# A planner's priorities replaced by a table of ranks, and a weight load tied to the other operand of pair 4

## The chip, the cores and the metric

The kernel runs on one core of one Trainium2 chip. The metric is the device time of one execution in microseconds (us); the shorter, the better. Three runs of the kernel before gave 262.81, 263.26 and 263.25 us, median 263.25.

## What is computed

The reference is a sparse attention followed by a feed-forward layer. There are 4 batches, 8 heads, 768 positions and a head size of 64.

```
k_rep = k.reshape(B, H, 12, 64, D).mean(axis=3)        # one mean key per block of 64
gate  = q @ k_rep^T, causal by blocks                   # each query picks its 3 best blocks and its own
attn  = softmax(mask(0.125 * q @ k^T))                  # only picked blocks, and causal
x     = (attn @ v) as 3072 tokens x 512
out   = gelu_tanh(x @ w_in) @ w_out                     # 512 -> 2048 -> 512, fp32 out
```

## The kernel before, in words

Heads are handled in pairs, four pairs to a batch, sixteen in all; pairs 0 to 3 are batch 0. Each pair goes through these steps.

- **Loads** (`load`, issued on the queue of SyncE, SP): k, q and v of the pair. In batch 0 they arrive as they lie, most of them in rooms inside the tiles G and TS; from pair 4 on k and q arrive in a layout that VectorE can transpose in blocks (`emit_t`, L278). Pair 0 is loaded in halves by `load_0` (L303) from two queues.
- **Preparation** (`pre`): in batch 0 TensorE turns k and q with an identity matrix (L417, L420). Block sums of k give gate scores (L542). VectorE adds the constant cgate (L565), takes the eight largest (L574), compares with the third (L575), and combines the result with the constant ownm into an additive mask (L579). TensorE or a DMA transposes the mask (L611, L618), and it is copied into place (L247, L243). The constants come from `consts` on GpSimd (POOL): cgate and ownm in `gates` (L354 to L365), block indicators in `e16` (L372, L375), and four sets of memsets (L383 to L387), one for each of four buffers.
- **Heads**: scores into a two-bank PSUM tile called wide (L715 in `heads2` for batch 0, L898 in `heads` for the others), exp on ScalarE (L734, L911), a causal select on the diagonal by POOL (L760, L925), the product with v (L783, L937), normalisation on VectorE (L801, L802; L820, L821), and a transpose into xT (L840, or the DMA of L845). There are two wide tiles and six buffers for the exponentials (`at`).
- **Stage one** (`s1`): x @ w_in, 128 matmuls of 384 columns to a batch (L973), with gelu on ScalarE (L985) into G. It shares the two wide tiles with the scores.
- **Stage two**: for batch 0 plain (`s2_plain`, L1055, 96 matmuls). The plain matmuls of the first output tile need the first half of w_out from their first step on. Batches 1 to 3 use a scheme with seven products instead of eight (`s2`, L1103, 168 matmuls to a batch), whose sums VectorE makes (`sums` L1043, `w_sums` L1025) and whose results it joins (L1147).

The table of exp and that of gelu are switched by a small activation (L681); ScalarE does it twice to a batch.

**Weights and queues.** `load_w` (L333, L336) is issued by POOL. Ahead of the first half of each weight it copies 16 elements of a tile of the last load it is to follow (L333, the tiles `after_in` and `after_out`): POOL waits there until that load has landed, and what stands behind it in POOL's order waits too. w_in follows v of pair 3, w_out follows k of pair 4. `hold` (L344) puts a tiny DMA on SP's queue that reads the first half of a weight, so that SP issues nothing further until it has landed: held_in stands before the loads of pair 4, held_out before the later ones. `fill` (L393) issues eight DMAs on SP that copy the block indicators under kT.

**The order of the work.** No order is written by hand. Every step is an `Op` with its engines and a planned duration on each, its dependencies, the buffers that it takes and gives, and a priority. `Plan.solve` is a list scheduler: at each turn it looks at all steps that could start, keeps those that start within 0.03 us of the earliest, and takes the one with the lowest priority number (a planned DMA goes by the time at which it became ready). The plan's start times then give the order in which instructions are emitted, and each engine runs its own instructions strictly in that order. Buffers, and the engine of steps that may run on several, are chosen by the plan as well. Priorities in the kernel before are formulas, such as `1000 * b + 600 + n` for stage one and `1e6` for `warm`.

`warm` (L1200) adds 72 matmuls of 256 columns with an identity whose results nobody reads. Their priority is the worst, so that the plan puts them where TensorE would find nothing else; all 72 are always emitted, and each takes a PSUM bank for its time.

Of the kernel before, what the change touches and what calls it, by code (L numbers as in the profile page):

```python
# [15 lines left out]
MASKVAL = 28672.0  # L16
NEGBIG = -1.0e9
SCALE = 0.125


class Op:
# [13 lines left out]
class Plan:  # L35
# [12 lines left out]
    def add(self, *a, **kw):  # L48
        op = Op(*a, **kw)
        self.ops.append(op)  # L50
        return op
# [81 lines left out]
def kernel(  # L133
# [16 lines left out]
    HP = H // 2  # L150
# [59 lines left out]
    for i in range(NB):  # L210
# [3 lines left out]
                     for h in range(2)])  # L214
# [3 lines left out]
    plan = Plan({  # L218
        **{kind: ([tuple(persist.tile([128] + dims, dt, name=f"{kind}_{n}_{m}")
                         for m, (dims, dt) in enumerate(parts))  # L220
                   for n in range(most)], most)
           for kind, most, parts in (
               ("at", 6, [([1024], FP16)]),
               ("osb", 2, [([2, 2, HD], FP32)]),
               ("ksd", PF, [([NC * 2 * 64], FP32)]),
               ("qsd", PF, [([NC * 2 * 64], FP32)]),
# [24 lines left out]
    ld = {}  # L251
# [75 lines left out]
    def load_w(name, dst, src, part, deps, prio, after=None):  # L327
        view = src.rearrange("(i p) f -> p i f", p=128)

        def emit(_):  # L330
            if after is not None:
                x = const.tile([1, 16], FP32, name=f"after_{name}")
                nc.gpsimd.tensor_copy(out=x, in_=T[after][0:1, 0, 0, 0:16]  # L333
                                      if len(T[after].shape) == 4 else
                                      T[after][0:1, 0, 0:16])
            nc.gpsimd.dma_start(out=dst[part], in_=view[part])  # L336
        go = add({POOL: 1.0}, emit, deps, prio=prio)
        issued[name] = go
        return add({"DMA": 6.0}, lambda _: None, [go], prio=prio, lag=1.6)

    def hold(name, src, dep):
        def emit(_):
            x = const.tile([1, 16], FP16, name=f"held_{name}")
            nc.sync.dma_start(out=x, in_=src[0:1, 0, 0:16])  # L344
        return add({SP: 0.5}, emit, [dep], prio=-1)
# [350 lines left out]
    def heads2(p):  # L696
# [3 lines left out]
        for ui, unit in enumerate(units(p)):  # L700
# [30 lines left out]
            def ex_e(_, u=u, n=n):  # L731
# [5 lines left out]
                        "p (h w) -> p h w", h=2)[:, :, 0:n],  # L737
                    func=AF.Exp, bias=0.0, scale=SCALE)
            ex = add({ACT: 0.13 + 2 * n * 0.000833}, ex_e,
# [137 lines left out]
    def heads(p):  # L877
# [4 lines left out]
        for h in range(2):  # L882
            pvs = []
            for gi, (ja, jb) in enumerate(groups):
# [24 lines left out]
                def ex_e(_, u=u, n=wa + wb):  # L909
# [3 lines left out]
                        in_=plan.buf[("st",) + u][:, 0:n],  # L913
                        func=AF.Exp, bias=0.0, scale=SCALE)
                ex = add({ACT: 0.84}, ex_e,
# [279 lines left out]
    def warm():  # L1195
        z = ident16.unsqueeze(1).to_broadcast([128, 2, 128])
        on = add({"NONE": 0.0}, lambda _: None, [], -1e6, lag=1.3)
        for n in range(NWARM):
            def emit(_, n=n):
                nc.tensor.matmul(plan.buf["warm", n][:, 0:256], ident16, z,  # L1200
                                 start=True, stop=True)
            add({PE: 0.215 if n < NCOLD else 0.107}, emit, [on], 1e6,
                takes=("warm", ("warm", n)),
                gives=[("warm", n)])
# [24 lines left out]
    for x in range(2):  # L1229
        w_ready["out", x] = load_w(  # L1230
            "out", w_out16, moe_w_out,
            (every, slice(NF // 2 * x, NF // 2 * (x + 1)), every),
            [ld["k", HP]], 40, None if x else ("k", HP))
    held.append(hold("out", w_out16, w_ready["out", 0]))
    for p in range(HP):
        heads2(p)
# [12 lines left out]
    for p in range(HP, NPAIR):  # L1249
# [4 lines left out]
        if hp == HP - 1:  # L1254
            s1(b)
            s2(b)
    warm()
    order = plan.solve()
    with tc.manual_schedule():
        for op in order:  # L1260
# [31 lines left out]
```

## Time and profile before

| What | us |
|---|---|
| median of three runs | 263.25 |
| time of the profiled execution | 262.67 |
| its span in the profile | 261.0 |
| TensorE busy (matmul) | 253.7 |
| TensorE weight loads | 176.2 |
| VectorE busy | 177.8 |
| ScalarE busy | 164.4 |
| GpSimd busy | 80.8 |

The span is the time from the first to the last thing that the profiler saw on the core; what the profiled execution took beyond it lies around it. A row such as "40.43 0.83 PE L1200 MATMUL ... x6" of the timeline is: start, length of the run of equal instructions, engine, line of the kernel, operation, tiles, count. In a row of groups the numbers behind the bar are busy time, mean of one instruction in ns, and idle time of the engine just before them with what ended it. In the table of stages each engine has its busy time and, in brackets, its instructions; the last three columns are the granted clock of TensorE, the share of the DMA engines and GB/s.

### The profile page before, as it was taken

Reading aid. Unit: us, or ns where it says so; the run is one execution under the profiler, and the core shown is the slowest. Engines: PE = TensorE matmul, PEld = TensorE weight load, DVE = VectorE, ACT = ScalarE, POOL = GpSimd, SP = SyncE. Lnnn points to the kernel's source line nnn. Section 1 sums busy time; section 2 is a strip of 40 time slices with the busy share of each in tenths; the row PEclk is TensorE's granted clock in tenths of the full one; section 3 lists DMA queues with packets and bytes.
Section 4 is the critical chain, followed back from the end, with each engine's and each line's share of the span. In section 5 each row is a group of like instructions: output and inputs, shape, how many; then the busy total and the mean of one; then the engine's idle time right before and its main releaser. Section 6 shows DMA issues by size and latency. Waiting matters only on the chain.

```text
span 261.0 us, 6531 instructions
## 1 busy us (share of the span) xinstructions
PE 253.7 (97%) x2542; PEld 176.2 (68%) x2542; DVE 177.8 (68%) x527; ACT 164.4 (63%) x207; POOL 80.8 (31%) x165
## 2 busy tenths in 40 slices
PE   6999999999999999999999999999999999999994
PEld 5777776565564655656677888656777887656883
DVE  2978737506598999989988999997534353345543
ACT  2366887666898696575799920666899912665000
POOL 8657634002374383120057820200044400000000
PEclk9999999999999999999999999999999999999999
DMA  8997999999999999899979913211004122000222
GB/s 163 219 215 148 187 194 134 178 185 192 163 194 173 190 189 203 156 179 164 178 124 169 193 56 116 97 28 25 3 1 143 34 80 84 0 0 3 80 83 80
DMA packets 130816, 32.63 MB, mean 125 GB/s; under 512 B 124544, under 2 KB 126688, under 8 KB 130784
## 3 DMA queue, kind: packets, MB, share of 16 engines
q1 hardware_dynamic: 126048, 27.62, 53.0%
q0 software_dynamic: 3136, 4.19, 9.9%
q10 hardware_dynamic: 1600, 0.39, 0.8%
q8 instruction: 20, 0.33, 0.5%
q14 instruction: 12, 0.10, 0.1%
HBM read 27.26 MB, written 6.29 MB: 129 GB/s over the span
## 4 chain that ended last, share of the span: by engine, by line
PE 85%; ACT 6%; DVE 6%; issue 2%; POOL 1%; DVEq 0%; POOLq 0%; ACTq 0%
PE wide L973 32%; PE bank L1103 20%; PE wide L898 7%; PE bank L1055 7%; ACT at L911 5%; PE bank L937 5%; PE bank L1200 3%; PE wide L715 3%; PE bank L542 2%; PE bank L783 2%; PE bank L420 1%; PE bank L417 1%; PE bank L840 1%; PE bank L611 1%; POOL at L925 1%
## 5 line engine op out<-in xcount | busy, mean ns | idle before, releaser
L973 PE MATMUL wide<-xT,w_in 128*128 128x384 f16 x512 | 85.9, 326 | 0.0
L985 ACT ACTIVATE G<-wide 128x768 f16<-128x768 f32 x64 | 51.8, 810 | 40.0 <-PE wide L973 40.0
L973 PEld LDWEIGHTS <-w_in 128*128 128x128 f16 x512 | 49.4, 98 | 32.7 <-issue 1.5
L911 ACT ACTIVATE at<-wide 128x896 f16<-128x896 f32 x72 | 60.7, 915 | 3.6 <-PE wide L898 2.2
L925 POOL TENSOR_SCALAR_AFFINE_SELECT at<-at 128x256 f16<-128x256 f16 x72 | 29.7, 416 | 64.1 <-ACT at L911 63.3
L898 PE MATMUL wide<-qT,kT 76*128 76x512 f16 (+1 forms) x192 | 38.9, 305 | 0.3 <-DVE qT L247 0.2
L1147 DVE TENSOR_TENSOR osb<-bank,osb 128x512 f32<-128x512 f32 (+1 forms) x36 | 22.3, 619 | 12.9 <-PE bank L1103 12.8
L1103 PEld LDWEIGHTS <-G 128*128 128x128 f16 x288 | 27.3, 98 | 5.2 <-issue 0.3
L1103 PE MATMUL bank<-w_out,G 128*128 128x256 f16 x216 | 30.5, 272 | 0.0
L937 PEld LDWEIGHTS <-at 128*128 128x128 f16 x504 | 23.6, 97 | 5.9 <-POOL at L925 1.8
L734 ACT ACTIVATE at<-wide 128x1024 f16<-128x1024 f32 (+3 forms) x24 | 21.2, 917 | 9.1 <-PE wide L715 8.8
L937 PE MATMUL bank<-v,at 128*128 128x65 f16 x504 | 26.5, 194 | 0.1
L1055 PE MATMUL bank<-w_out,G 128*128 128x512 f16 x96 | 25.1, 379 | 0.4 <-DVE osb L247 0.4
L245 POOL CAST kT<-k 64x768 f16<-64x768 f32 x17 | 14.4, 845 | 29.1 <-DVE k L436 28.6
L1103 PEld LDWEIGHTS <-XS 128*128 128x128 f16 x216 | 20.5, 98 | 3.4 <-DVE XS L1043 0.2
L898 PEld LDWEIGHTS <-kT 76*128 76x128 f16 x192 | 15.6, 97 | 9.7 <-issue 1.4
L1103 PE MATMUL bank<-TS,XS 128*128 128x256 f16 x144 | 20.3, 272 | 0.0
L1043 DVE TENSOR_TENSOR XS<-G 128x768 f16<-128x768 f16 x12 | 6.5, 552 | 18.1 <-ACT G L985 18.1
L436 DVE STREAM_TRANSPOSE k<-ksd 128x768 f32<-128x768 f32 x12 | 11.5, 962 | 9.1 <-DMA ksd<-in_k_dram 9.0
L245 POOL CAST v<-vsd 128x768 f16<-128x768 f32 x13 | 11.1, 851 | 18.6 <-DMA vsd<-in_v_dram 18.6
L1200 PE MATMUL bank<-ident 128*128 128x256 f16 x72 | 12.3, 302 | 2.1 <-DVE ident L175 2.1
L821 DVE TENSOR_TENSOR xn<-bank,zr 128x384 f16<-128x384 f32 x24 | 13.4, 558 | 0.8
(99 smaller groups left out, 323.8 us busy)
## 6 DMA issues: line engine op xcount, KB each, us to landing
out_dram<-osb SPq DMA_DIRECT2D x24, 256.0 KB
vsd<-in_v_dram SPq DMA_DIRECT2D x26, 192.0 KB
ksd<-in_k_dram SPq DMA_DIRECT2D x48, 96.0 KB
qsd<-in_q_dram SPq DMA_DIRECT2D x48, 96.0 KB
w_in<-in_moe_w_in_dram POOLq DMA_DIRECT2D x2, 1024.0 KB, 10.7
w_out<-in_moe_w_out_dram POOLq DMA_DIRECT2D x2, 1024.0 KB, 12.7
G<-in_k_dram SPq DMA_DIRECT2D x4, 192.0 KB
G<-in_q_dram SPq DMA_DIRECT2D x4, 192.0 KB
```

Source lines behind the costliest of these rows:

```text
L245: nc.gpsimd.tensor_copy(out=out, in_=in_)
L734: nc.scalar.activation(out=T["at", u][:, :, 0:n], in_=plan.buf[("st",) + u].rearrange("p (h w) -> p h w", h=2)[:, :, 0:n], func=AF.Exp, bi ...
L898: nc.tensor.matmul(st[:, x:e], kT16[i][h][0:76, s0:s0 + 128], qT16[i][h][0:76, s0 + (x - cb):s0 + (e - cb)], start=True, stop=True)
L911: nc.scalar.activation(out=T["at", u][:, 0:n], in_=plan.buf[("st",) + u][:, 0:n], func=AF.Exp, bias=0.0, scale=SCALE)
L925: nc.gpsimd.affine_select(out=dg, in_=dg, compare_op=ALU.is_ge, fill=0.0, base=0, pattern=[[0, 2], [1, 128]], channel_multiplier=-1)
L937: nc.tensor.matmul(pvv[:, qc, 0:65], at[:, cb + (qc - jc) * 128: cb + (qc - jc + 1) * 128], v16[i][:, jc, h, :], start=(gi == 0 and jc == ...
L973: nc.tensor.matmul(hps[:, 512 * e:512 * e + HALF], w_in16[:, ci, (2 * j + e) * 128: (2 * j + e + 1) * 128], T["xT", b][:, ci, HALF * h:HAL ...
L985: nc.scalar.activation(out=G[:, :, h, j, :], in_=plan.buf["hps", b, j, h].rearrange("p (e w) -> p e w", e=2)[:, :, 0:HALF], func=AF.Gelu_a ...
L1055: nc.tensor.matmul(plan.buf["ops", b, ti], G[:, f % 2, 2 * ti // NC, f // 2, ti % (NC // 2) * 128:ti % (NC // 2) * 128 + 128], w_out16[:, ...
L1103: nc.tensor.matmul(dst[:, HD * h:HD * h + HD], FACT[m][0][:, j, t * 128:(t + 1) * 128], FACT[m][1][:, j, :], start=(clear and j == 0), sto ...
L1147: nc.vector.tensor_tensor(out=dst(), in0=src(), in1=other(), op=ALU.add)
L1200: nc.tensor.matmul(plan.buf["warm", n][:, 0:256], ident16, z, start=True, stop=True)
```

## The change

A list of integers, RANK, is put at the head of the file, one for each step of the plan in the order in which the steps are added. After all steps have been added, each step's priority is overwritten with its rank; the last 72, the fillers, all have the worst rank, 1684. The scheduler, the planned durations and the steps themselves stay. The ranks come from a search made outside the kernel, which also replayed each plan with late loads.

The dependency of the w_out load, and the tile that `after_out` reads, become q of pair 4 in place of k of pair 4. In the code q of a pair is added after k.

```diff
+RANK = [
+    186, 144, 143, 173, 141, 142, 315, 164, 439, 154, 164, 553, 307, 165,
...
+    1684, 1684, 1684, 1684]
...
         w_ready["out", x] = load_w(
             "out", w_out16, moe_w_out,
             (every, slice(NF // 2 * x, NF // 2 * (x + 1)), every),
-            [ld["k", HP]], 40, None if x else ("k", HP))
+            [ld["q", HP]], 40, None if x else ("q", HP))
     held.append(hold("out", w_out16, w_ready["out", 0]))
...
     warm()
+    assert len(RANK) == len(plan.ops)
+    for op, rank in zip(plan.ops, RANK):
+        op.prio = rank
     order = plan.solve()
```

A line of the kernel before stands 147 lines further down in the kernel after, and 150 behind the new loop.

## The prediction

> **What bounds the kernel now.** I read the page's busy shares first, then the chain that ended last, then the table of stages, then the timeline.
>
> ```profile
> span 261.0 us, 6531 instructions
> PE 253.7 (97%) x2542; PEld 176.2 (68%) x2542; DVE 177.8 (68%) x527; ACT 164.4 (63%) x207; POOL 80.8 (31%) x165
> PEclk9999999999999999999999999999999999999999
> DMA  8997999999999999899979913211004122000222
> PE 85%; ACT 6%; DVE 6%; issue 2%; POOL 1%; DVEq 0%; POOLq 0%; ACTq 0%
> L1200 PE MATMUL bank<-ident 128*128 128x256 f16 x72 | 12.3, 302 | 2.1 <-DVE ident L175 2.1
> ```
>
> The reader is to see that TensorE carries both the busy time and 85% of the chain, at full clock, and that 72 of its matmuls (L1200) compute nothing: they multiply an identity and are never read. Because matmul ends are modelled, I measured PE from start to start. A row of twelve of them ends 1.47 us after it begins and a single one takes 0.27, so the pitch is (1.47 - 0.27)/11 = 0.109 us; the 48 stage-one matmuls of L973 that take 7.96 us give (7.96 - 0.33)/47 = 0.162. The stages:
>
> ```profile
> 10.00:20.00 10.00, 9.91 (x142) 7.51 (x142) 7.95 (x39) 6.31 (x9) 5.37 (x12) 1.00 1.18 217
> 20.00:30.00 10.00, 9.90 (x166) 7.36 (x164) 8.06 (x30) 7.04 (x9) 7.76 (x13) 1.00 0.85 150
> 90.00:103.00 13.00, 13.00 (x122) 7.31 (x122) 12.71 (x22) 11.23 (x15) 7.40 (x12) 1.00 0.97 187
> 103.00:127.00 24.00, 24.00 (x174) 14.32 (x172) 22.48 (x83) 15.00 (x20) 3.31 (x4) 1.00 1.00 170
> 185.00:207.00 22.00, 22.00 (x295) 17.45 (x293) 10.94 (x25) 21.35 (x27) 9.09 (x23) 1.00 0.19 53
> ```
>
> Columns: PE, PEld, DVE, ACT and POOL busy, clock, DMA share, GB/s. From 41 us on PE issues almost without a break. Where it lacks useful work the fillers stand:
>
> ```profile
> 40.43 0.83 PE L1200 MATMUL bank<-ident 128*128 128x256 f16 x6
> 113.40 0.82 PE L1200 MATMUL bank<-ident 128*128 128x256 f16 x6
> 127.74 1.28 ACT L681 ACT_TABLE_LOAD   x1
> 128.57 1.47 PE L1200 MATMUL bank<-ident 128*128 128x256 f16 x12
> ```
>
> So an order that has less to fill makes the stream shorter, and the same 72 instructions then stand elsewhere. PE waits that the profile names are tiny (2.1 us at the start, 0.6 later).
>
> **What the Trainium skill says.** "Perfetto Trace Analysis", Identifying the Most-Contended Engine: matmul busy share says little about the distance to the limit, LDWEIGHTS busy share more. Here 97% against 68%, which is why I use pitches. "TensorE: Matmul & The Clock Gate", Part 1: warm pitch is N/2.4 GHz plus about 2.5 ns, half speed returns after an idle window of about 3.4 us. The pitch agrees (256 columns: 109 ns); no fall-back is in this trace, and the gap I expect below is shorter than that. "DMA: Bandwidth & Descriptors", Issuing engines are not separate DMA queues: SP's and GpSimd's transfers interleave on the same engines. The trace agrees: from 30 to 50 us the share stays at 1 while both move data.
>
> **The change, part by part.** The numbers in RANK replace every priority; operations and their counts stay, and the built program has as many PE matmuls as before. What moves:
>
> *Fillers.* Before, the built order puts 52 of 72 ahead of the bulk of stage one of batch 0, 8 inside stage one of batch 1, 12 at the switch to exp at 128.6. After, it puts 34 ahead of that bulk, 4 before the last 154 stage-two matmuls, and 34 behind the last useful one. Off the path: 34 x 0.109 = 3.71 us. What keeps PE busy instead is named by the order: behind stage one of batch 1 stand blocks of 10, 10 and 22 stage-two matmuls where the 12 fillers were, and stage one of batch 0 starts (16 matmuls, 2.6 us) between the last value matmuls. The tail: the last fillers wait for the last two osb additions (0.69 us), then 25 run, 0.7 + 25 x 0.109 + 0.3 = 3.7 us after the last useful matmul; today the output takes 261.0 - 257.1 = 3.9 us from there. Cost 0, at worst 0.3.
>
> *Gate constants.* cgate and ownm move on POOL from first place to last, behind four sets of memsets and E.
>
> ```profile
> 1.43 0.36 POOL L355 TENSOR_SCALAR_AFFINE_SELECT cgate<-cgate 128x120 f32<-128x120 f32 x1
> 4.84 1.87 POOL L375 TENSOR_SCALAR_AFFINE_SELECT G<-G 64x768 f16<-64x768 f16 x2
> 8.57 0.21 DVE L565 TENSOR_TENSOR sel<-sel,cgate 128x48 f32<-128x48 f32 x1
> 10.96 0.10 PEld L715 LDWEIGHTS <-XS 64*128 64x128 f16 x2
> ```
>
> One memset set takes 1.28 us (2.74 to 4.02), E 2.74, the constants 1.8. From 0.95: four sets and E, 7.86, 0.25 for the identity and 0.6 for its own memset and select give cgate at about 9.7 and ownm at 10.8. The first selection (L565), now at 8.57, starts at 9.8, its last step waits for ownm and ends at 11.0; mask transpose 11.2; DVE's queue has a query cast (0.76) and a transpose ahead of the mask copy, so the first scores come at about 12.5 instead of 10.96. At equal work (24 key/query turns, 16 score matmuls, 5 mask transposes) I get 14.7 against 13.4, with two fillers fewer: +1.5 us. Bounds: 0 if the PE work pulled forward (the pair-1 query turn) had to be paid anyway and ACT catches up (it idles 9.1 us before the exps of L734), +2.5 if ACT's lag stays. I take 1.5. The identity itself comes 0.4 us later (a madd memset of 0.64 goes ahead); that lies under the same wait.
>
> *SP's loads.* v of pair 2 moves behind v of pair 3 and the eight fills of kT.
>
> ```profile
> 17.90 1.47 SPq L267 DMA_DIRECT2D TS<-in_v_dram  x2
> 21.24 6.25 SPq L393 DMA_DIRECT2D kT<-G  x8
> 22.83 0.83 POOL L245 CAST v<-TS 128x768 f16<-128x768 f32 x1 [0.62 <-DMA TS<-in_v_dram]
> 24.42 1.66 POOL L336 DMA_DIRECT2D w_in<-in_moe_w_in_dram  x2
> ```
>
> Issue moves from 17.9 to 19.4 + 6.25 = 25.7, where w_in runs. Alone it lands about 4.9 us after its issue begins (17.9 to 22.8), sharing with w_in some 6.6: 30.6 to 32.3. Its cast stands on POOL ahead of three selects of pair 2, and PE needs pair 2's values once all 48 scores of that pair are out, about 33. Between 0 and +2; I take 0.5. Out writes of batch 0 stand three loads earlier in SP's queue, but the first is ready at about 64 (16 plain matmuls and a copy), before its turn at some 65: 0.
>
> *The w_out wait* (after_out) now reads q of pair 4. In the code q follows k, but the new order issues q first on SP, so it still waits for the first of the two: about 0, at most 2.6 (the query issue at 38.5). Behind it on POOL are pair 4's kT and v casts, not due for 15 us. w_out's first half lands 10.3 us after issue (51.4 before). With v of pair 2 ahead of w_in that becomes 53 to 54; the first plain stage-two matmul moves from behind all 128 stage-one matmuls to behind 76, about 40.9 + 13.4 = 54.3. Bounds 0 and +2; I take 0.3.
>
> *Heads of batches 1 to 3.* In the profile the score groups of the last two batches follow each other at 0.815 us, ACT's pace, over 0.80 us of PE work. The new order spreads each 24 over 26 to 29 us of PE work: gain up to 24 x 0.015 x 2 = 0.7, and loss where DVE (98% busy from 90 to 103) meets an earlier PE. I take -0.5, bounds -0.7 and +1.5.
>
> Sum: -3.71 + 1.5 + 0.5 + 0.3 - 0.5 = -1.9 us. Against the profiled execution, 262.67 (span 261.0 and 1.67 around it), 260.8; the median of the runs is 0.58 higher, so 263.25 - 1.9 = 261.3.
>
> **Rivals.** *Full gain*: the early wait is made good before 41 us, because ACT has 9.1 us of idle to give there, and nothing else is late: 263.25 - 3.7 - 0.5 = 259.1. For it: a PE order with nothing to fill. Against: cgate at 9.7 delays the whole chain. *Slower, the values of pair 2*: place, POOL's cast of v behind a landed load, with three selects and PE's value matmuls queued behind it. From 33 us each microsecond of lateness is one of PE. It turns the balance to slower when v is usable 2.5 us later than I count, a landing past 34.8; at 35.9 the time is 263.25 - 1.9 + 3.6 = 264.9. For it: w_in takes half the engines then. Against: 4.9 us from issue when alone. *Nothing gained*: DVE, 35.2 of 37 us busy from 90 to 127, becomes the bound; PE arrives earlier and waits, and about 1.8 us come back: 263.2. Against: stage two of batch 1 now starts later in the order, behind all of its stage one. That the new w_out wait does nothing by itself is part of the forecast.
>
> **How the numbers follow.** Forecast 0.54, full gain 0.20, nothing gained 0.10, slower 0.16. A measurement here tells 0.2%, 0.53 us, from no change. Faster: 0.54 + 0.20 less a little = 0.73; same 0.11; slower 0.16. The range takes full gain at its best side and slower short of its far end: 258.8 to 264.2; forecast alone 260.2 to 262.4.
>
> **What would show it.** Fillers: L1200 rows after the last stage-two matmul, none at 113 and 128. First L715 near 12.5. First plain stage-two matmul without a PE wait on a DMA. Score groups of batches 2 and 3 wider apart than 0.82. Wrong if L715 starts at 11 (constants cost nothing), if PE stands before the value matmuls of pair 2, or if gaps of PE add up to more than 3.7 us.

## The result and the profile after

The kernel after takes 271.99 us (median of four runs, 271.48 to 273.31) against 263.03 us before: the ratio is 1.0349, 95% interval 1.031 to 1.0388. It is slower by about 9 us, where 261.3 was predicted and 264.2 was the top of the range. Its profiled execution took 273.31 us, with a span of 271.6.

The page of the kernel after, in the lines that answer to those shown of before: span, busy shares, the granted clock and the DMA share in 40 slices, and the chain that ended last.

```profile
span 271.6 us, 6511 instructions
...
PE 255.8 (94%) x2542; PEld 178.0 (66%) x2542; DVE 173.5 (64%) x520; ACT 167.8 (62%) x211; POOL 86.2 (32%) x168
...
PE   6899904999999999999999999999999999999997
PEclk9999975799999999999999999999999999999999
...
DMA  8994995079979989999989696112110242000212
...
PE 83%; DMA 7%; POOL 4%; SPq 2%; ACT 2%; issue 1%; DVE 1%; POOLq 0%; DVEq 0%; ACTq 0%
```

A slice is 6.8 us. In the sixth, from 34 to 41 us, TensorE stands still (the 0 in its row), and in that slice and the next two the granted clock is down to 0.7, 0.5 and 0.7: these were all 9 before. The chain now holds 7% of DMA. From the eighth slice on, TensorE is as full as before. So one place holds the loss. Who waited for whom, TensorE's own list:

```profile
PE bank L930 <- POOL at L907: 10.7, 1, 10.7
PE bank L1347 <- DVE ident L322: 2.3, 1, 2.3
PE bank L758 <- DVE madd L726: 0.5, 1, 0.5
```

One wait of 10.7 us, at a value matmul of batch 0 (L930, L783 before), for a select on GpSimd (L907). What the select waited for is in the timelines (start in us, duration in us, engine, line, operation; in brackets the time waited and the releaser). First SP's queue:

```profile
20.29 6.27 SPq L540 DMA_DIRECT2D kT<-G  x8
26.60 1.35 SPq L414 DMA_DIRECT2D TS<-in_v_dram  x2
```

GpSimd, where the first half of w_in goes out and the cast and selects follow:

```profile
25.34 0.92 POOL L483 DMA_DIRECT2D w_in<-in_moe_w_in_dram  x1
...
42.19 0.83 POOL L392 CAST v<-TS 128x768 f16<-128x768 f32 x1 [12.08 <-DMA TS<-in_v_dram]
42.97 1.58 POOL L907 TENSOR_SCALAR_AFFINE_SELECT at<-at 128x512 f16<-128x512 f16 x3
```

And TensorE, at the value matmuls:

```profile
44.25 1.06 PE L930 MATMUL bank<-v,at 128*128 128x65 f16 x16 [10.71 <-POOL at L907]
```

v of pair 2 is issued at 26.6 us, behind the eight fills, 1.3 us after w_in. It has landed at 42.2 us, 15.6 us after its issue began; before, it took 4.9 from issue to cast. The cast stood 12.1 us, three selects stood behind it, and TensorE behind those. Its sixteen matmuls then take 1.06 us, at half the clock; sixteen took 0.68 at 28.4 us.

How the two transfers shared the engines is seen in the DMA view of the kernel after between 32 and 37 us (packets and MB of each queue; q0 carries w_in, q1 is SP's):

```profile
q0 software_dynamic: 450, 0.89, 93.8%
q1 hardware_dynamic: 453, 0.12, 17.5%
```

As many packets of one as of the other, but w_in's have 2,048 bytes and those of v 256. SP's queue gets about one eighth of what w_in gets.

The turns are not the whole of the 15.6 us. The view from 27 to 30 us has one line of a queue with data, and none of SP's:

```profile
q0 software_dynamic: 218, 0.45, 105.3%
```

The first of v's packets starts at 30.8 us, 4.2 us after the issue. From then to 39 us, when w_in's packets run out, the queues take turns, and about half of v's 1,536 packets go through. The other half follows in 1.7 us, by 40.7, and the last share lands at 42.1.

### The profile page after: what moved, and what is told of

Read it like the earlier page. It is cut to its first block, busy times and chain, and to the rows that moved or that the text cites. A ratio compares the mean times of both kernels' runs of the same rounds, so it can differ in the third digit from the quotient of the medians.

```text
span 271.6 us, 6511 instructions
## 1 busy us (share of the span) xinstructions
PE 255.8 (94%) x2542; PEld 178.0 (66%) x2542; DVE 173.5 (64%) x520; ACT 167.8 (62%) x211; POOL 86.2 (32%) x168
## 4 chain that ended last, share of the span: by engine, by line
PE 83%; DMA 7%; POOL 4%; SPq 2%; ACT 2%; issue 1%; DVE 1%; POOLq 0%; DVEq 0%; ACTq 0%
PE wide L1120 31%; PE bank L1250 20%; PE wide L1045 9%; PE bank L1202 6%; DMA TS<-in_v_dram 5%; PE bank L1084 5%; PE wide L862 2%; PE bank L1347 2%; SPq L540 2%; PE bank L930 2%; PE bank L689 2%; PE bank L564 1%; DMA vsd<-in_v_dram 1%; POOL madd L531 1%; PE bank L987 1%
## 5 line engine op out<-in xcount | busy, mean ns | idle before, releaser
L1120 PE MATMUL wide<-xT,w_in 128*128 128x384 f16 x512 | 87.7, 326 | 0.0
L1058 ACT ACTIVATE at<-wide 128x896 f16<-128x896 f32 x72 | 62.7, 916 | 9.6 <-PE wide L1045 7.0
L1072 POOL TENSOR_SCALAR_AFFINE_SELECT at<-at 128x256 f16<-128x256 f16 x72 | 31.1, 436 | 58.8 <-ACT at L1058 58.3
L1045 PE MATMUL wide<-qT,kT 76*128 76x512 f16 (+3 forms) x192 | 38.1, 305 | 0.2
L1294 DVE TENSOR_TENSOR osb<-bank,osb 128x512 f32<-128x512 f32 (+1 forms) x36 | 22.2, 619 | 12.1 <-PE bank L1250 11.8
L392 POOL CAST kT<-k 64x768 f16<-64x768 f32 x20 | 17.8, 889 | 33.3 <-DVE k L583 30.8
L1084 PEld LDWEIGHTS <-at 128*128 128x128 f16 x504 | 22.0, 98 | 4.1 <-issue 0.3
L1045 PEld LDWEIGHTS <-kT 76*128 76x128 f16 x192 | 17.3, 98 | 10.7 <-issue 0.7
L1084 PE MATMUL bank<-v,at 128*128 128x65 f16 x504 | 23.9, 194 | 0.0
L930 PE MATMUL bank<-v,at 128*128 128x65 f16 x168 | 8.8, 208 | 10.7 <-POOL at L907 10.7
L1190 DVE TENSOR_TENSOR XS<-G 128x768 f16<-128x768 f16 x12 | 7.4, 624 | 14.5 <-ACT G L1132 14.3
L705 DVE STREAM_TRANSPOSE sel<-bank 128x160 f32<-128x160 f32 (+2 forms) x17 | 5.5, 335 | 16.9 <-PE bank L689 16.5
L930 PEld LDWEIGHTS <-at 128*128 128x128 f16 x168 | 7.4, 107 | 12.4 <-POOL at L907 10.9
## 6 DMA issues: line engine op xcount, KB each, us to landing
out_dram<-osb SPq DMA_DIRECT2D x24, 256.0 KB
w_in<-in_moe_w_in_dram POOLq DMA_DIRECT2D x2, 1024.0 KB, 11.6
```

The costliest lines, as they stand in the source:

```text
L392: nc.gpsimd.tensor_copy(out=out, in_=in_)
L930: nc.tensor.matmul(pvv[:, c, h, 0:65], at[:, h, col:col + 128], v16[i][:, jc, h, :], start=one, stop=False, skip_group_check=True)
L1045: nc.tensor.matmul(st[:, x:e], kT16[i][h][0:76, s0:s0 + 128], qT16[i][h][0:76, s0 + (x - cb):s0 + (e - cb)], start=True, stop=True)
L1058: nc.scalar.activation(out=T["at", u][:, 0:n], in_=plan.buf[("st",) + u][:, 0:n], func=AF.Exp, bias=0.0, scale=SCALE)
L1072: nc.gpsimd.affine_select(out=dg, in_=dg, compare_op=ALU.is_ge, fill=0.0, base=0, pattern=[[0, 2], [1, 128]], channel_multiplier=-1)
L1084: nc.tensor.matmul(pvv[:, qc, 0:65], at[:, cb + (qc - jc) * 128: cb + (qc - jc + 1) * 128], v16[i][:, jc, h, :], start=(gi == 0 and jc == ...
```

## The experiments

Theory A: the late landing of v of pair 2, through its place behind the fills and beside w_in, is the whole loss, and the rest of the new order gains. Theory B: the new order stalls as a whole, and this is only its largest stall. Theory C: GpSimd's order, with the cast ahead of three selects, is what stopped TensorE. Most edits move one step in the list of instructions after the plan has been made, so that nothing else changes (in the edits shown, words in place of code stand for the steps that are looked up):

```
    def move(op, ref, behind=False):
        order.remove(op)
        order.insert(order.index(ref) + behind, op)
```

### The load alone moved back

```diff
     order = plan.solve()
+    move(issued["v", 2], first of the eight fills in order)
```

> The kernel after, with one load moved: v of pair 2 is issued on SP ahead of the eight fills instead of behind them; nothing else in any queue changes. Theory A (position of that load): it lands before 27 us, TensorE's wait of 10.7 us at 33 us is gone, the clock stays full, and the time is 271.99 - 10.7 - about 1.5 for the slow clock = 259.8, at most 261.5, faster than before. Theory B (the new order as a whole stalls, this load is only the largest of many): 264 or more. Theory C (GpSimd's queue, with the cast of those values ahead of three selects): no different from A here.

Measured: 260.35 us (260.0 to 261.06), ratio to before 0.9897, interval 0.9875 to 0.9919. TensorE's waits in this kernel:

```profile
PE bank L1347 <- DVE ident L322: 2.3, 1, 2.3
PE bank L758 <- DVE madd L726: 0.9, 1, 0.9
PE bank L1347 <- DVE sel L705: 0.8, 1, 0.8
```

The wait of 10.7 us is gone, the clock is at 9 in every slice. One load's place in one queue is worth 271.99 - 260.35 = 11.6 us: 10.7 of waiting and about 0.9 more. Between the two profiled executions (273.31 and 261.06) it is 12.2, so the rest is 0.9 to 1.5 us; the slow clock is its likely cause, but no run shows that by itself. Theory B falls: all that is left of the new order is 2.7 us faster than before.

### The same load moved back in the kernel before

```diff
     order = plan.solve()
+    for op in [issued["v", 3]] + the fills:
+        move(op, issued["v", 2])
```

> The kernel before with one thing of the new order alone: v of pair 3 and the eight fills are issued on SP ahead of v of pair 2; all priorities and all other queues stay. Theory A: its packets of 256 bytes then alternate one for one with w_in's of 2,048, about 90 of each in a microsecond, it lands near 42 us, TensorE stops some 9 to 11 us at pair 2's first value matmul (30.7 us before) and the clock falls: 272 to 275. Theory B (the new order as a whole is what stalls): the old order has slack for the load, 263 to 266.

Measured: 270.62 us, ratio 1.0278, interval 1.0236 to 1.0319, below the range expected. The place alone makes the old order slow as well. The way to it was another than expected, as GpSimd's timeline shows:

```profile
29.93 0.83 POOL L245 CAST v<-TS 128x768 f16<-128x768 f32 x1 [7.26 <-DMA TS<-in_v_dram]
30.71 0.64 POOL L760 TENSOR_SCALAR_AFFINE_SELECT at<-at 128x512 f16<-128x512 f16 x1
...
31.42 1.66 POOL L336 DMA_DIRECT2D w_in<-in_moe_w_in_dram  x2
```

And TensorE's:

```profile
31.40 0.40 PE L783 MATMUL bank<-v,at 128*128 128x65 f16 x4 [5.82 <-POOL at L760]
```

In the old order the cast stands ahead of the w_in load on GpSimd, so w_in waited for v, the two did not meet, and v landed 3.6 us after its issue at 26.4. TensorE stopped for 5.8 us, not 9 to 11, with the clock down to 0.7 in two slices. It did not stop for v of pair 2 itself. The matmuls at 31.40 are those that stood at 25.22 before; they belong to pair 1, and pair 2's values start later (30.67 before). They waited for a select that stood on GpSimd behind the waiting cast. In the old order, then, the late load reaches TensorE by the way that theory C names.

### The cast out of the way of the selects

```diff
     order = plan.solve()
+    move(ld["v16", 2], first value matmul of pair 2)
```

> The kernel after, with the cast of v of pair 2 moved on GpSimd behind three more selects, to just ahead of the first use; the load stays behind the fills. Theory A: TensorE still needs the values, so it waits till the load has landed at 42 us; at most 1 us is gained, 271 to 272. Theory C: the selects queued behind the cast were what stopped the stage, and most of the 10.7 us go: 264 or less.

Measured: 271.81 us, ratio 1.0329, interval 1.0292 to 1.0366. TensorE waits 8.7 us, now for the cast itself:

```profile
PE bank L930 <- POOL v L392: 8.7, 1, 8.7
```

Theory C falls for the new order. The selects behind the cast cost two of the microseconds waited, but the median is only 0.2 us below the kernel after; where the rest went is not shown.

### The w_in load after the values

```diff
     order = plan.solve()
+    move(both halves of the w_in load, ld["v16", 2], behind=True)
```

> The kernel after, with the w_in load moved on GpSimd behind the cast of v of pair 2, so that v of pair 2, still behind the eight fills, has the DMA engines to itself. If w_in's competition is what made 15 us of its landing, it lands 4 to 6 us after its issue, near 31.5 us, and TensorE's wait at 33 us falls under 1 us; w_in then lands near 41 and 45 us, stage one starts about there and w_out follows 7 us later, so that the time is 263 to 268 for another reason. If the place behind the fills alone makes it late, it lands near 40 us as before and the time stays at 272 or above.

Measured: 269.62 us (two executions, 267.63 and 271.62, at mean granted clocks of 0.994 and 0.981; ratio 1.0246, interval 1.0141 to 1.0351). One lies in the range expected, the profiled one above it. But the question was when v lands. The DMA view from 27 to 30 us has 1,592 packets of SP's queue and 0.41 MB: the load runs through in 3 us with no w_in beside it, its first packet 1.2 us after the issue at 26.46, and has landed at 30.0. Its cast starts at 32.31, right behind the select ahead of it, and not for want of data:

```profile
32.31 0.83 POOL L392 CAST v<-TS 128x768 f16<-128x768 f32 x1
33.08 0.19 POOL L480 COPY after_in<-vsd 1x16 f32<-1x16 f32 x1
...
34.74 1.66 POOL L483 DMA_DIRECT2D w_in<-in_moe_w_in_dram  x2 [1.48 <-issue]
...
49.15 0.19 POOL L480 COPY after_out<-qsd 1x16 f32<-1x16 f32 x1 [3.71 <-DMA qsd<-in_q_dram]
```

So w_in made the load late, not the fills alone: they delay the issue by 6.3 us, w_in the landing by some 12. TensorE still waits 2.0 us for pair 2's selects. The time stays high because w_in and w_out are late in turn: TensorE waits 3.9 us for w_out, and the clock falls to 0.5 in a slice behind that wait. In this execution it was low near 14 us too.

### Smaller packets of w_in

```diff
-            nc.gpsimd.dma_start(out=dst[part], in_=view[part])
+            for cut in the two halves of part's columns:      # w_in alone
+                nc.gpsimd.dma_start(out=dst[cut], in_=view[cut])
```

> The kernel after with each half of the w_in load cut into two of half the columns, so that its packets are 1,024 bytes and not 2,048. Between 30 and 38 us the kernel after moves 727 packets of w_in and 666 of SP's queue. If the two queues alternate packet for packet, the queue of v of pair 2 gets about 1.4 to 1.7 times as many packets a microsecond in that stretch (950 to 1,100), and w_in about as many again, at half the bytes. If SP's queue has a fixed rate beside the other, it stays near 670; if the bytes were shared, both would have been even. The time itself may change little, 269 to 273, since w_in lands later.

Measured: 270.67 us (ratio 1.0289, interval 1.0263 to 1.0316). The DMA view from 32 to 37 us, to be laid beside the one of the kernel after:

```profile
q0 software_dynamic: 770, 0.77, 90.8%
q1 hardware_dynamic: 771, 0.19, 29.7%
```

Again one for one, at 1.7 times the number. From 30 to 38 us SP's queue moves 1,537 packets, above the 950 to 1,100 expected, since v ran alone for a part of a microsecond, between two pieces of w_in, at the start. The cast starts at 39.98 and not at 42.19. For the stretch in which both queues move, a fixed rate of SP's queue and an even share of bytes are both excluded.

### The gate constants first again

```diff
     order = plan.solve()
+    move(issued["v", 2], first of the eight fills in order)
+    move(c_E["gates"], order[0])
```

> As the run before, and the gate constants are made first on GpSimd again, as in the kernel before. If the late constants cost what the prediction took, this is 1.5 us below the run with the load alone, and the first score matmul starts near 11 us instead of 12.2. If ScalarE makes the delay good before stage one starts, it is within 0.3 us of it.

Measured: 259.96 us (259.83 to 260.22), ratio 0.988, interval 0.9863 to 0.9898, 0.4 us below the run with the load alone; the intervals of the two overlap, so the size is uncertain. The first selection starts at 9.48 instead of 9.91 and the first score matmul at 11.50 instead of 12.66. Stage one then starts at 39.23 instead of 40.38, earlier by the same 1.15 us: the delay was not made good on the way, although ScalarE's idle time ahead of its exps fell from 6.3 to 4.6. But the profiled execution with the load alone is the slowest of its four (261.06). In two other traces with late constants, the kernel after and the run with the copy on k below, the first scores stand at 12.03 and 12.15, so that the delay is more often 0.5 to 0.7 us.

### The wait for w_out

In the kernel before, only the tile that the copy ahead of w_out reads:

```diff
-            [ld["k", HP]], 40, None if x else ("k", HP))
+            [ld["k", HP]], 40, None if x else ("q", HP))
```

> The kernel before with the w_out edit alone: the copy ahead of the w_out load reads q of pair 4, the second of the two on SP in this order, so here the load does wait for the whole pair. The plan and all queues are the same. It is issued about 2.5 us later and lands near 54 and 59 us; the first matmul that reads w_out stands at 63.6 us. No change: 263.2, within 0.3.

Measured: 263.01 us, ratio 0.999, interval 0.9981 to 1.0. No change.

In the kernel after, with the load moved back, the copy reads the operand that this order issues second:

```diff
+    move(issued["v", 2], first of the eight fills in order)
-            [ld["q", HP]], 40, None if x else ("q", HP))
+            [ld["q", HP]], 40, None if x else ("k", HP))
```

> The kernel after with v of pair 2 ahead of the fills, and the copy ahead of the w_out load reads k of pair 4, which the new order issues second, so that the load waits for the whole pair. Against the run with the load alone moved (260.35): w_out is issued about 2.2 us later, its first half lands near 54 us in place of 51.9, and the first plain stage-two matmul stands at 54.0: TensorE waits 0 to 1 us there, 260.3 to 261.3. If the wait matters more than that, the plain matmuls wait again at the second half, and it is over 261.3.

Measured: 260.53 us (260.25 to 260.92), ratio 0.9896, interval 0.9881 to 0.991, within the spread of the run with the load alone (260.35). The copy starts at 42.61 instead of 42.01, not 2.2 us later: GpSimd's last select of pair 3 is done at 41.7, and the load of k lands 0.9 us behind that. With q the copy followed the select at once. TensorE does not wait at the first plain matmul (53.7 us). So the w_out edit does nothing that can be measured in either kernel.

### The fillers

In the kernel before, the last 34 fillers moved behind everything, and then left out:

```diff
     order = plan.solve()
+    for op in fillers[38:]:
+        order.remove(op)
+        order.append(op)          # the second kernel has no such line
```

> The kernel before with only its last 34 fillers moved behind the last stage-two matmul; every other instruction stays in its place. If the fillers stand in gaps that exist anyway, as the prediction took, TensorE waits where they stood and the time is 262.6 to 263.3. If fillers delay useful work by themselves, up to 3.7 us go: 259.5 to 261.

Measured: 264.3 us, ratio 1.0049, interval 1.0037 to 1.0062: slower than before by 1.2 us, which neither side expected. Twelve of them had stood at the switch to exp; there TensorE now waits for ScalarE as long as they took, and at the end stands what was moved:

```profile
128.96 0.54 PE L898 MATMUL wide<-qT,kT 76*128 76x512 f16 x2 [1.36 <-ACT at L911]
...
254.95 1.04 PE L1103 MATMUL bank<-w_out,G 128*128 128x256 f16 x8
...
256.77 3.87 PE L1200 MATMUL bank<-ident 128*128 128x256 f16 x34 [0.78 <-DVE osb L1147]
```

The last useful matmul ends at 256.0, 1.1 us earlier than before, so some 2.6 of 3.7 us of fillers had stood in gaps that exist. But the row of fillers ends at 260.6, and the span 1.4 us behind it.

> The kernel before without its last 34 fillers, all else in place. With them moved behind the last stage-two matmul it took 264.3, its useful stream ending 1.1 us earlier. If the tail of fillers hid that gain, this takes 262.0; if the fillers cost nothing where they stood, 263.1.

Measured: 262.44 us, ratio 0.998, interval 0.9964 to 0.9996. Without the row at the end the same stream takes 1.9 us less.

The twenty executions fall in two groups. Fifteen have a mean granted clock of 0.997 or more and a median of 261.98; five have 0.990 to 0.993 and a median of 263.61. The trace is one of the five. In it TensorE waits 1.36 us at the switch to exp, where twelve fillers had stood, and from 130 to about 134 us the granted clock is 0.5. With the fillers moved to the end five of twenty are at 0.994; of the 23 executions of the kernel before that were taken beside these runs, none is below 0.997. So it seems that the fillers at this switch also kept the clock up.

The same in the new order, with both moves above:

```diff
     order = plan.solve()
+    move(issued["v", 2], first of the eight fills in order)
+    move(c_E["gates"], order[0])
+    for op in fillers[38:]:
+        order.remove(op)
```

> The kernel after with v of pair 2 ahead of the fills and the gate constants first, and without the 34 fillers that stand behind the last useful matmul. The prediction took these at nothing. In that kernel's trace with them the last useful matmul ends at 252.5 us and the span at 258.3, 5.8 us later; before, that tail took 3.9. If the fillers hold the end, the tail goes back to about 3.9 and the time from 259.96 to about 258.1; if the tail is the output's own, it stays at 260.0, within 0.3.

Measured: 257.93 us (257.82 to 258.17), ratio 0.9808, interval 0.9791 to 0.9824. This is 2.0 us below the same kernel with them, and the fastest of the study, 1.9% under the kernel before.

```profile
span 256.1 us, 6444 instructions
...
PE 249.4 (97%) x2508; PEld 172.7 (67%) x2508; DVE 173.8 (68%) x520; ACT 167.7 (65%) x211; POOL 86.1 (34%) x168
...
PE 92%; DVE 5%; ACT 1%; issue 0%; DVEq 0%; ACTq 0%
```

That is its page: TensorE is busy for 97% of the span, and DMA is gone from the chain.

## Why the prediction was wrong

**The step that failed** is "SP's loads". The prediction had the issue right (25.7 against 26.6 us), the queue behind it right (cast, three selects, TensorE from about 33; the last score matmul ahead of the wait is at 33.3), and the competitor right, but it let the load take "sharing with w_in some 6.6" us, "30.6 to 32.3", and took 0.5 us for it, bounds 0 and 2. It landed at 42.2. How the 6.6 was reached is not told; the slower rival's "w_in takes half the engines then" points to an even share of the engines, but the queues share turns. The Trainium skill says so in "DMA: Bandwidth & Descriptors", Queues, rings and completion order: each DMA engine goes round the queues at packet granularity. The counts agree, 450 to 453 and 770 to 771. The page's packet holds several descriptors, typically 9 to 17; counts over 5 us do not tell whether the engines change after each of the profile's packets or after equal groups of them. The prediction had cited the same page for the fact that transfers interleave, and had not asked how large the packets were. Nor did its trace show how two queues share: between 30 and 50 us both moved data, but mostly one after the other (from 32 to 36 us, 420 packets of w_in and none of SP's).

Against the 3.6 us that the load took alone, the trace gives the 12 us of lateness in parts. About 3 passed before the first packet, 4.2 us after the issue and not 1.2. About 7 went to the turns: half of the packets took 8.2 us, and 1.0 without w_in. The other half and the landing of the last share took the remaining 2. Why SP's queue moved nothing from 27 to 30 us, while w_in's packets ran, no run says; the kernel before shows the same at w_in's start (28 to 29 us, 104 packets to none), where no load that was needed soon stood in it.

**The slower rival was the case.** It named the place and the price, one microsecond of TensorE for each of lateness, with the turn at a landing past 34.8. Its own rule, put at 42.2, gives 263.25 - 1.9 + 9.9 = 271.25; measured were 271.99. That this comes so close is in part luck, since other terms of the sum were off as well (below). It had 0.16, and its landing of 35.9 was far too early, for the reason above.

**The clock.** The prediction said that the gap it expected was shorter than the idle window of the clock gate, which was right for that gap. The gap of 10.7 us was not: TensorE stops at 33.5 us, the granted clock is 0.5 from about 37 until about 50.5, and sixteen value matmuls take 1.06 us in it. The fall after some 3.4 us of standing is as "TensorE: Matmul & The Clock Gate", Part 1, has it. The page gives about 3.4 us of sustained work for the way back; here 6.3 passed from the first matmul at 44.25. Nor is a gap shorter than the page's idle window always safe: in the kernel before without its last 34 fillers the clock fell in the traced execution behind a wait of 1.36 us.

**Fillers.** Mechanism and count were right: in the new order 34 of them are not needed, 3.71 us, and with the load and the constants moved the last useful matmul ends at 252.4 us against 257.1, 4.7 us earlier. That fillers mostly fill gaps that exist holds too (1.1 of 3.7 us came back when they were moved in the old order). The size that was off is the tail, "cost 0, at worst 0.3": it cost 2.0 us. The last fillers end 3.7 us after the last useful matmul, as worked out (though without the wait for the additions: all 34 run in one row). The step failed in comparing this with the 3.9 us to the end of the span, since the span does not end with TensorE's last matmul. It ended 1.8 us behind the last filler in the kernel after, and 1.4 in the kernel before with the fillers moved. What fills that time is not shown.

**Gate constants.** The times were right (selection 9.91 against 9.8, first scores at 12.0 to 12.7 against 12.5), the cost was not: 0.4 and not 1.5 us. The low end of the bounds was nearer, but not because ScalarE catches up. The prediction compared 12.5 with the old order's 10.96; in the new order the first scores stand at 11.50 even with the constants early, and what is left of the delay lasts until stage one.

**The w_out wait** was right: q goes first in the new order, so that the wait is for the first of the two, and even waiting for the second costs nothing that can be measured. The first plain matmul stood at 54.0 us in the kernel with the load moved (54.3 predicted), its weights landed near 51.9; the 0.3 taken for it is 0.

**Heads.** The gain of 0.5 there was not tried by itself and stays open. The traces agree with it: from 56 us to the last useful matmul TensorE is idle for 0.95 us in the kernel before and for 0.18 us with both moves.

**The sum.** For the new order without the late load the prediction's own terms give -1.9 - 0.5 = -2.4 us; measured was the ratio 0.9897, which is -2.7 of 263.25. Part of the agreement is luck: with the measured sizes in place of its terms for the tail (+2.0), the constants (-1.1) and w_out (-0.3) the sum would be -1.8, so that some 0.9 us more came out of the stream than was taken, and no run says where.

## What to carry to other kernels

When a load with small packets is put beside one with large packets, price it by turns and not by bytes: for as long as the other queue has packets, it moves only as many as that queue does. Here it also started 3 us late. A filler that nobody reads is free only where something else ends later, so count the end of the program too; and one that stands in a gap may be keeping the clock up as well. An order that leaves nothing to fill also leaves nothing to absorb a late transfer: before trusting one, find the first consumer of each moved load and what stands behind it on every engine.

## What the runs showed of the hardware

- Two queues that both moved data alternated one packet for one packet, 450 and 453 in 5 us at 2,048 and 256 bytes, 770 and 771 at 1,024 and 256. Before that SP's queue moved nothing from 27 to 30 us, while w_in's moved 218 packets. A load of 393 KB in 256-byte packets took 15.6 us from issue to landing in that company and about 3.6 alone.
- After 10.7 us of standing, TensorE ran its matmuls at a granted clock of 0.5 from 44 until about 50.5 us. In one execution a wait of 1.36 us was followed by 0.5 for about 3.4 us.
- A row of matmuls that nobody reads, at the end of the program, held its end by 1.9 to 2.0 us. The span ended 1.4 us behind the last of them in the kernel before with 34 of them moved there, and 1.8 in the kernel after.
